# Half-array slots with one PSUM bank per half for the value blocks and a projection of the first nine units of a gated attention kernel

## The chip, the cores and the metric

The kernel runs on one core of one Trainium2 chip. The metric is the device time of one execution in microseconds, the median of several runs; less is better. An engine is named as the profile names it: PE (TensorE's matmuls), PEld (its weight loads), DVE (VectorE), ACT (ScalarE), POOL (GpSimd), SP (SyncE, which issues the DMAs here).

## The reference, cut to what matters

```python
def _A_ref(x, wqkv, wo):                     # x: 1 x 2048 x 512, 32 heads of 16, window 256
    q, k, v = split_heads(x @ wqkv)
    scores = einsum("bhqd,bhkd->bhqk", q, k) * 16 ** -0.5
    scores = where(0 <= i - j < 256, scores, -1e9)
    return merge_heads(softmax(scores) @ v) @ wo

def _B_ref(x, w_gate, w_up, w_down):         # hidden width 1376
    return (sigmoid(x @ w_gate) * (x @ w_up)) @ w_down

g = sigmoid((x * gate_w).sum(-1))
out = g * _A_ref(...) + (1 - g) * _B_ref(...)
```

All data are float32. Every product is computed from operands that are split in a high part (rounded to the fast matmul type fp32r) and a low part (the rest), as high x high + high x low + low x high. So a product over 512 inputs is 4 x 3 = 12 matmuls of 128 rows.

## The kernel before, in words

**Stages.** First x and the weights of the value product are loaded and split, seven of the sixteen value blocks (`v_block`, L416: 128 tokens each) and the first query/key projections (`proj`, L410: 512 tokens of a group of four heads) are computed. Then comes the main loop over `u` (L597). Unit `u` is a block of 128 queries of a group of four heads. For each of the four heads `hh`, `s_part` (L295) computes scores of the queries against at most three blocks of keys, and VectorE finds each row's maximum in one instruction (L311, out `junk`, with a read of the accumulator behind it). Nine units later (`LAG`), with the maxima added in by way of DRAM (`max_split` L318, `max_store`, `max_load`), `st_part` (L343) computes the scores again, transposed and less their maximum, ScalarE takes the exponent, and two units later `pv_part` (L375) adds the product with the values into the bank `pv`. All `s` and `st` matmuls contract over 64 rows only; they use one half of the array's rows, heads 0 and 2 the lower one, 1 and 3 the upper one, so that two of them can run at once. Each takes a bank of `s` (two buffers) or `st` (two buffers; in the first nine units, heads 2 and 3 of `s_part` use those).

**What fills TensorE.** Between the attention matmuls stand those of gate/up and of the projections of later groups (`turns`, L527), in half-array slots: a matmul over 128 rows is cut into one over rows 0 to 63 and one over rows 64 to 127, which add into the same bank (tag `misc`, three buffers) one after the other, 18 slots apart, each beside a half of another group. This starts with unit 9.

**The first nine units** have no `st` and no `pv`. What fills them is a list `first` (L498): the nine value blocks that are left, and the projection 5, appended in unit 5 (L625), 12 slots each. `run_first` (L513) issues them after the four `s_part` of a unit, as whole 128-row matmuls, about 13 per unit. A value block ends with ScalarE's copy from its bank into V (L227; V holds 17 columns per head, the last of them ones); the projection ends with ScalarE's rounding to `sh` and VectorE's low part `sl` (L253, L261), copied by SP's DMAs into the `ring` that the attention reads. In unit 8 the value blocks end, the first gate/up weights are split (L654: they take the place of the value weights), and the projection's 12 matmuls close the stage.

**What sets the order.** PE, ACT, SP and DVE run in the order in which the program calls them. Three lists move work: `behind` (VectorE's steps, emptied after each `s_part` in the first nine units and one per head later), `acts` (ScalarE's), `later` (DMAs). Semaphore waits are put in by the framework wherever a buffer or a value is needed; an instruction that waits holds all that is behind it on its engine.

**The bank `pv`** is cleared at the very start by two matmuls with zeros (L174 to L177), behind 14 others that warm up TensorE (L172), and later by a VectorE memset of 256 columns after each take (L401).

## Time and profile before

| | |
|---|---|
| runs | 753.11 us median of 3 (752.37 to 753.42) |
| the profiled execution | 751.81 us; span of its instructions 750.1 us |
| granted TensorE clock | 1.00 throughout |
| busy share of the span | PE 99%, PEld 78%, DVE 64%, ACT 58%, POOL 23% |
| first instruction to the first s matmul | 0 to 40.94 us |
| units 0 to 8 | 40.94 to 75.16 us |
| first pv matmuls (unit 12) | from 84.83 us |

A row of the trace in order of time has the start in us, the length in us, the engine, the line of the kernel, the operation, out<-in with the shapes, the count, and in brackets the idle time before it with what ended that. Lengths of matmuls overlap, since they are pipelined: their pace is read from one start to the next. Some matmul records are missing from the trace, so rows are picked where the sequence is whole. A row of a stretch has its limits, its length, and the busy time and count of PE, PEld, DVE, ACT and POOL, then the granted clock and the DMA figures. A row of a group has the busy time in us and the mean ns of one behind the bar.

### The profile page before, as it was taken

The numbers are of one execution on the slowest core, as the hardware profiler recorded it, in microseconds if no ns is written. First come the engines' busy times: TensorE is split into PE (matmuls) and PEld (weight loads), VectorE is DVE, ScalarE is ACT, GpSimd is POOL, SyncE is SP. The second block draws the span as 40 slices with busy tenths as digits, with TensorE's granted clock in tenths as the row PEclk, the third lists the DMA queues.
The fourth block names the chain that finished last, engine by engine and source line by source line (L and its number), as shares of the span: only waits on it lengthen the run. The fifth ranks groups of instructions, "written<-read, shape, count | busy, mean of one in ns | idle before, by whom it ended". The sixth has DMA issues, their size and how long they took to land.

```text
span 750.1 us, 17420 instructions
## 1 busy us (share of the span) xinstructions
PE 744.0 (99%) x6180; PEld 581.5 (78%) x6180; DVE 482.0 (64%) x1455; ACT 435.5 (58%) x927; POOL 171.9 (23%) x256
## 2 busy tenths in 40 slices
PE   8999999999999999999999999999999999999997
PEld 6877777787777877778787787778866888888886
DVE  5346767776776766776677676677613776657371
ACT  6422666666676667666667666666656663525241
POOL 7000233233233233323323333332331000000000
PEclk9999999999999999999999999999999999999999
DMA  8340434426344353443543426443355967557451
GB/s 305 96 113 19 105 98 124 127 68 181 113 114 125 109 154 105 122 112 108 153 122 92 125 71 177 125 130 102 109 187 176 290 209 233 170 194 223 128 150 56
DMA packets 69959, 103.58 MB, mean 138 GB/s; under 512 B 19314, under 2 KB 29042, under 8 KB 69872
## 3 DMA queue, kind: packets, MB, share of 16 engines
q1 hardware_dynamic: 69872, 102.48, 46.3%
q8 instruction: 48, 0.79, 0.4%
q14 instruction: 39, 0.32, 0.2%
HBM read 45.26 MB, written 32.00 MB: 103 GB/s over the span
## 4 chain that ended last, share of the span: by engine, by line
PE 97%; DMA 1%; DVE 1%; issue 0%; SPq 0%; ACT 0%; DVEq 0%
PE gu L237 34%; PE pv L384 12%; PE pj L237 11%; PE s L305 7%; PE st L351 5%; PE pd L71 5%; PE pd L73 5%; PE pd L72 5%; PE vps L71 2%; PE pa L73 2%; PE pa L71 2%; PE pa L72 2%; PE vps L73 2%; PE vps L72 2%; DMA V<-in_xT_dram 1%; DVE junk L311 0%
## 5 line engine op out<-in xcount | busy, mean ns | idle before, releaser
L311 DVE CUSTOM_DVE_ANT_0 junk<-s,mask 128x384 f32<-128x384 f32 (+2 forms) x512 | 272.1, 531 | 140.1 <-PE s L305 78.2
L237 PE MATMUL gu<-xh,w 64*128 64x512 f32 (+2 forms) x1384 | 344.4, 392 | 0.0
L356 ACT ACTIVATE pt<-st 128x384 f32<-128x384 f32 (+2 forms) x512 | 242.4, 474 | 169.3 <-PE st L351 69.8
L237 PE MATMUL gu<-xl,w 64*128 64x512 f32 (+3 forms) x692 | 227.4, 392 | 0.0
L237 PEld LDWEIGHTS gu<-xh,w 64*128 64x128 f32 (+2 forms) x1384 | 190.1, 183 | 19.3 <-issue 0.4
L361 POOL TENSOR_SCALAR_AFFINE_SELECT pt<-pt 128x512 f32<-128x512 f32 x128 | 88.1, 688 | 382.3 <-ACT pt L356 382.3
L351 PE MATMUL st<-ring 64*128 64x384 f32 (+2 forms) x536 | 170.2, 332 | 0.0
L305 PE MATMUL s<-ring 64*128 64x384 f32 (+2 forms) x536 | 165.8, 332 | 0.1
L305 PEld LDWEIGHTS s<-ring 64*128 64x128 f32 x536 | 94.4, 184 | 39.3 <-DVE nm L321 12.9
L237 PEld LDWEIGHTS gu<-xl,w 64*128 64x128 f32 (+3 forms) x692 | 107.9, 183 | 5.7
L351 PEld LDWEIGHTS st<-ring 64*128 64x128 f32 x536 | 97.1, 184 | 12.2 <-issue 2.7
L237 PE MATMUL pj<-xh,wqh 64*128 64x512 f32 (+1 forms) x232 | 91.1, 397 | 0.3 <-ACT xh L67 0.2
L384 PE MATMUL pv<-pt,V 128*32 128x384 f32 (+2 forms) x1408 | 91.0, 388 | 0.0
L237 PE MATMUL pj<-xl,wqh 64*128 64x512 f32 (+1 forms) x232 | 90.1, 393 | 0.4 <-DVE xl L68 0.4
L366 POOL TENSOR_SCALAR_AFFINE_SELECT pt<-pt 128x512 f32<-128x512 f32 x112 | 74.2, 663 | 0.0
L237 PE MATMUL pj<-xh,wql 64*128 64x512 f32 (+1 forms) x232 | 70.9, 392 | 0.0
L71 PE MATMUL pd<-ring,hb 128*128 128x512 f32 (+1 forms) x176 | 69.3, 394 | 0.0
L73 PE MATMUL pd<-ring,hb 128*128 128x512 f32 (+1 forms) x176 | 68.9, 392 | 0.0
L72 PE MATMUL pd<-ring,hb 128*128 128x512 f32 (+1 forms) x176 | 68.4, 389 | 0.0
L384 PEld LDWEIGHTS pv<-pt,V 128*32 128x32 f32 x1408 | 37.2, 109 | 36.0 <-issue 29.7
L67 ACT CAST hb<-V 128x512 fp32r<-128x512 f32 (+1 forms) x44 | 27.4, 622 | 63.9 <-DVE V L565 51.4
L479 ACT COPY sp<-gu 128x512 f32<-128x512 f32 (+2 forms) x88 | 51.1, 582 | 2.0 <-PE gu L237 2.0
(74 smaller groups left out, 898.5 us busy)
## 6 DMA issues: line engine op xcount, KB each, us to landing
gu_scratch<-sp SPq DMA_DIRECT2D x80, 256.0 KB
V<-gu_scratch SPq DMA_DIRECT2D x80, 256.0 KB
ring<-sh SPq DMA_DIRECT2D x128, 128.0 KB
ring<-sl SPq DMA_DIRECT2D x64, 128.0 KB
guraw<-in_wgu_dram SPq DMA_DIRECT2D x20, 256.0 KB
V<-in_xT_dram SPq DMA_DIRECT2D x16, 256.0 KB
oT_scratch<-ob SPq DMA_DIRECT2D x128, 32.0 KB
xl<-oT_scratch SPq DMA_DIRECT2D x16, 256.0 KB
```

The source lines that it names most:

```text
L71: mm(ps, lh, rh, start=first, stop=False)
L72: mm(ps, lh, rl, start=False, stop=False)
L73: mm(ps, ll, rh, start=False, stop=last)
L237: mm(pt[0:fw], (wl if w == 2 else wh)[r, d], (xl if w == 1 else xh)[r, d, c * CH:(c + 1) * CH], start=k == 0 and half != 1, stop=k == 3 * ...
L305: mm(pt[:, (k - k0) * P:(e - k0) * P], lhsT, blk(g, k, hh, 1, e - k), start=k == k0, stop=e == i + 1, skip_group_check=True,)
L311: nc.vector.tensor_tensor_reduce(junk[:, 0:n], pt[:, 0:n], mask[:, 3 * P - n:], scale=1.0, scalar=NEG, op0=ALU.add, op1=ALU.max, accum_out ...
L351: mm(pt[:, (q - j) * P:(e - j) * P], lhsT, blk(g, q, hh, 0, e - q), start=q == j, stop=e == last, skip_group_check=True,)
L356: nc.scalar.activation(pts[u][:, hh, 0:n], pt[:, 0:n], AF.Exp, scale=SCALE)
L361: nc.gpsimd.affine_select(p[:, :, 0:P], p[:, :, 0:P], pattern=[[0, HG], [1, P]], compare_op=ALU.is_ge, fill=0.0, base=0, channel_multiplie ...
L366: nc.gpsimd.affine_select(p[:, :, 2 * P:], p[:, :, 2 * P:], pattern=[[0, HG], [-1, P]], compare_op=ALU.is_gt, fill=0.0, base=0, channel_mu ...
L384: mm(pv[32 * hh:32 * hh + 32, (q % 4) * P:(q % 4 + e - q) * P], V[:, j, h * VW:h * VW + 32], p[:, hh, (q - j) * P:(e - j) * P], start=Fals ...
L479: nc.scalar.copy(t[0:width(f, w)], gp.pop((f, c, w))[0:width(f, w)])
```

## The change

1. The two clearing matmuls on `pv` at the start go; the tile is made at unit 9 and cleared there by a VectorE memset of 512 columns. Until then its bank serves as a fourth bank for the value blocks and the projection.
2. A slot of a value block or of projection 5 is now two matmuls, one over rows 0 to 63 and one over rows 64 to 127, each into a bank of its own (`pair_of_banks`: in turn two of the three `misc` banks, and the third with `pv`).
3. The two banks are added: ScalarE copies the lower one to a tile, VectorE adds the upper one to it (`v_sum` into V; `proj_sum` into the tile, after which ScalarE rounds it to `sh` and VectorE computes `sl`).
4. The slots are issued after heads 1 and 3 of each unit (about seven at a time) and no longer all at the unit's end; in unit 8 only two are left for the first place and none for the second.
5. At the end of unit 8 `behind`, `soon` and `behind` are emptied after the projection, so that its sum, its rounding and its low part are in the queues ahead of unit 9.

```diff
-        pv = ps.tile([P, CH], F32, tag="pv", name="pv", bufs=1)
-        for k in range(2):
-            mm(pv[:, 2 * P * k:2 * P * k + 2 * P], warm[:, 0:P], warm[:, 0:2 * P],
-               start=k == 0, stop=True, skip_group_check=True)
...
-        first = [(ND, lambda d, b=b: v_part(b, d), lambda: None) for b in range(vnext, NB)]
+        def pair_of_banks(key):
+            if key not in halves:
+                tags = ("misc", "pv" if len(seen) % 2 else "misc")
+                seen.append(key)
+                halves[key] = [
+                    ps.tile([P, CH], F32, tag=t, name=f"{key}_{i}", bufs=3 if t == "misc" else 1)
+                    for i, t in enumerate(tags)
+                ]
+            return halves[key]
...
+        def v_slot(b, k, half):
+            d, w = divmod(k, 3)
+            r = slice(64 * half, 64 * half + 64)
+            bs = slice(b * P, (b + 1) * P)
+            mm(pair_of_banks(f"vh{b}")[half], (xl if w == 2 else xh)[r, d, bs], (wvl if w == 1 else wvh)[r, d],
+               start=k == 0, stop=k == 3 * ND - 1)
+
+        def v_sum(b):
+            lower, upper = halves.pop(f"vh{b}")
+            t = cpool.tile([P, CH], F32, tag="sp", name=f"vsum{b}", bufs=4)
+            nc.scalar.copy(t, lower)
+            heads = lambda v: v.rearrange("p (h w) -> p h w", w=DH)
+            behind.append(lambda: nc.vector.tensor_tensor(Vh[:, b, :, 0:DH], heads(upper), heads(t), op=ALU.add))
...
+        def proj_sum(s):
+            lower, upper = halves.pop(f"ph{s}")
+            t = cpool.tile([P, CH], F32, tag="sp", name=f"psum{s}", bufs=4)
+            nc.scalar.copy(t, lower)
+            pj[s] = t
+            behind.append(lambda: nc.vector.tensor_tensor(t, upper, t, op=ALU.add))
+            soon.append(lambda: proj_post(s))
...
         def run_first(n):
...
+                k, step, post = going[0]
+                for half in range(2):
+                    step(k, half)
...
             if u == LAG:
...
+                pv = ps.tile([P, CH], F32, tag="pv", name="pv", bufs=1)
+                nc.vector.memset(pv, 0.0)
...
                 if u < LAG:
                     flush(behind)
+                    if hh % 2 == 1:
+                        upto = min(n_first - 3 * ND, n_first * (2 * u + 1 + hh // 2) // (2 * LAG))
+                        run_first(upto - done)
+                        done = upto
...
-            if u < LAG - 1:
-                done += run_first(n_first * (u + 1) // LAG - done)
-            elif u < LAG:
-                run_first(n_first - done - 3 * ND)
+            if u < LAG:
+                flush(soon)
+            if u == LAG - 1:
                 split_gu(0, 0)
                 split_gu(0, 1)
                 flush(acts)
                 flush(behind)
                 run_first(3 * ND)
-                done = 0
+                flush(behind)
+                flush(soon)
+                flush(behind)
```

More of the change, by code (lines that the diff above doesn't have):

```diff
@@ L496, in proj_out, with proj_slot @@
             acts.append(lambda: (proj_hi(s), behind.append(lambda: proj_lo(s))))
-        first = [(ND, lambda d, b=b: v_part(b, d), lambda: None) for b in range(vnext, NB)]
+        halves = {}
+        soon = []
+        def pair_of_banks(key):
[7 more added lines that the diff above has]
+            return halves[key]
+        seen = []
+        def v_slot(b, k, half):
[10 more added lines that the diff above has]
+            behind.append(lambda: nc.vector.tensor_tensor(Vh[:, b, :, 0:DH], heads(upper), heads(t), op=ALU.add))
+        def proj_slot(s, k, half):
+            g, c = divmod(s, NC)
+            d, w = divmod(k, 2) if k < 2 * ND else (k - 2 * ND, 2)
+            r = slice(64 * half, 64 * half + 64)
+            mm(pair_of_banks(f"ph{s}")[half], wq[g][int(w == 2)][r, d], (xl if w == 1 else xh)[r, d, c * CH:(c + 1) * CH],
+               start=k == 0, stop=k == 3 * ND - 1)
+        def proj_sum(s):
[5 more added lines that the diff above has]
+            soon.append(lambda: proj_post(s))
+        first = [
+            (lambda k, h, b=b: v_slot(b, k, h), lambda b=b: v_sum(b)) for b in range(vnext, NB)
+        ]
         rest = [
@@ L513, in run_first @@
         def run_first(n):
-            done = 0
-            while done < n:
+            for _ in range(n):
                 if not going:
                     going.append([0, *(work or first).pop(0)])
-                k, count, step, post = going[0]
-                step(k)
-                done += 3 * ND // count
+                k, step, post = going[0]
+                for half in range(2):
+                    step(k, half)
                 going[0][0] += 1
-                if k + 1 == count:
+                if k + 1 == 3 * ND:
                     going.clear()
                     post()
-            return done
         def turns():
@@ L624, in gated_mix_kernel @@
                 if u < LAG:
-                    first.append((3 * ND, lambda k, s4=s4: proj_mm(s4, k), lambda s4=s4: proj_post(s4)))
+                    first.append((
+                        lambda k, h, s4=s4: proj_slot(s4, k, h), lambda s4=s4: proj_sum(s4)))
                 else:
@@ L658, in gated_mix_kernel @@
                 run_first(3 * ND)
-                done = 0
+                flush(behind)
+                flush(soon)
+                flush(behind)
             if u % 4 == 3 and u < NU:
```

## The prediction

> **What bounds the kernel now.** I read the page's first and fourth parts, then stretches of the trace, then TensorE's, VectorE's and ScalarE's instructions in order of time around the first nine units.

> ```profile
> span 750.1 us, 17420 instructions
> PE 97%; DMA 1%; DVE 1%; issue 0%; SPq 0%; ACT 0%; DVEq 0%
> 40.94:75.16 34.22, 34.22 (x158) 24.51 (x158) 21.34 (x81) 7.44 (x13) 0.00 (x0) 1.00 0.27 73
> ```

> The first two lines are the page's span and its chain by engine; the third is the stretch from the first s matmul to the first of unit 9 (length, then busy time of PE, PEld, DVE, ACT and POOL, granted clock 1.00). PE is never idle there, DVE is busy 21.34 of 34.22 us, ACT 7.44. So TensorE sets the time, and what the change can win must come out of PE's own sequence. In the built programs PE's instructions from unit 9 to the end are the same in the same order; SP's and POOL's are the same throughout. The change can therefore only shift the moment at which the rest begins.

> **What is removed: the seams between full-array and half-array matmuls.** One seam of before, in TensorE's order of time (start, length):

> ```profile
> 48.08 0.40 PE L73 MATMUL vps<-w,xl 128*128 128x512 f32 x1
> 48.41 0.62 PE L305 MATMUL s<-ring 64*128 64x384 f32 x4
> 48.96 0.50 PE L71 MATMUL vps<-w,xh 128*128 128x512 f32 x1
> 49.29 0.39 PE L72 MATMUL vps<-wvl,xh 128*128 128x512 f32 x1
> ...
> 52.09 0.40 PE L72 MATMUL vps<-wvl,xh 128*128 128x512 f32 x1
> ```

> From 49.29 to 52.09 lie twelve steps, 0.23 us each. Across the seam it goes slower: 0.33 before the four s matmuls, 0.55 for them, 0.33 after the first V matmul. What it would be without a seam stands in the later stage, where everything is half-array:

> ```profile
> 300.70 0.33 PE L305 MATMUL s<-ring 64*128 64x384 f32 x1
> 300.87 0.39 PE L237 MATMUL pj<-xh,wqh 64*128 64x512 f32 x1
> 300.87 0.39 PE L237 MATMUL gu<-xh,w 64*128 64x512 f32 x1
> 301.10 0.39 PE L237 MATMUL pj<-xl,wqh 64*128 64x512 f32 x1
> ```

> An s matmul takes its row group 0.17 us, and a pair of 512-column halves starts together and lasts 0.23: as long as one full-array matmul, so a pair costs no more than the one that it replaces. The seam's 1.21 us (48.08 to 49.29) become 0.23 + 2 x 0.17 + 0.23 = 0.80: 0.41 us per unit. For the stage: 120 slots (nine V blocks and one projection, twelve each) x 0.231 = 27.7, two s pairs in each of seven units 14 x 0.175 = 2.45, and four shorter ones, for which I take 0.185, 0.74; together 30.9 against 34.22. **Removed: 3.3 us** (from 0, if half slots keep the loss, to 3.8, if short s matmuls cost next to nothing). s is now issued as two pairs with some seven slots between them; with no seam that costs nothing.

> **What is added on the way: sums of two banks.** ACT copied each V block to V; now it copies one bank to a tile and VectorE adds the other. The nearest rows (groups of the stage, then of the whole span: busy us, mean ns):

> ```profile
> L227 ACT COPY V<-vps 128x512 f32<-128x512 f32 x9 | 5.3, 588 | 24.9 <-PE vps L73 24.9
> L263 DVE TENSOR_TENSOR sl<-pj,sh 128x512 fp32r<-128x512 f32 x1 | 0.7, 692 | 4.7 <-ACT sh L259 4.7
> L777 DVE SCALAR_TENSOR_TENSOR spare<-pa,gs,spare 128x512 f32<-128x512 f32 x16 | 12.0, 751 | 45.3 <-PE pa L73 44.1 <-ACT spare L773 1.2
> ```

> ACT's copy keeps its 0.59 us and has room. No row shows VectorE reading a bank and writing V's spaced rows. I take 0.69 (same operands but for the spacing, which the ACT copy, 588 ns, does not seem to feel), between 0.6 and the dearest of its kind, 0.75. Whether that is hidden is a matter of VectorE's pace:

> ```profile
> 70.06 0.56 DVE L311 CUSTOM_DVE_ANT_0 junk<-s,mask 128x384 f32<-128x384 f32 x1
> ...
> 70.66 0.17 DVE L321 TENSOR_SCALAR nm<-mx 128x16 fp32r<-128x16 f32 x1
> 70.87 0.18 DVE L322 SCALAR_TENSOR_TENSOR nm<-mx,nm 128x16 fp32r<-128x16 f32 x1
> 71.08 0.21 DVE L326 STREAM_TRANSPOSE nt<-nm 128x32 f32<-128x32 f32 x1
> ...
> 73.56 0.56 DVE L311 CUSTOM_DVE_ANT_0 junk<-s,mask 128x384 f32<-128x384 f32 x1
> ...
> 74.27 0.56 DVE L311 CUSTOM_DVE_ANT_0 junk<-s,mask 128x384 f32<-128x384 f32 x1
> ...
> 74.76 1.29 DVE L464 TENSOR_TENSOR w<-guraw,w 128x512 fp32r<-128x512 f32 x2
> 75.96 0.55 DVE L311 CUSTOM_DVE_ANT_0 junk<-s,mask 128x384 f32<-128x384 f32 x1
> ```

> Junk follows junk after 0.71 us, a tensor_tensor follows junk after 0.49, and each of two takes 0.60 until the next may start; max_split makes 0.71 into 1.23. A unit then asks 3 x 0.71 + 0.49 + 0.60 = 3.22 us of VectorE, and 13.3 x 0.231 + 0.35 = 3.43 of TensorE. It fits, with 0.2 to spare: **nothing** is added in units 0 to 8. The cover is thin: at the price 0.75 it still holds; if an add takes over 0.81 of VectorE's time, the rest is paid once per unit. Two banks per group alternate between four, so a group needs the bank of the last but one, given back by that add; it has one group's 2.8 us for it.

> **What is added at the end: a chain before unit 9.** Before, the last projection was rounded by ACT as unit 9 began and its low part came after unit 9's first junk. Now VectorE's order is: two gate/up low parts, the projection's sum, (ACT rounds it), its low part, the memset of the whole pv bank, and only then junk of unit 9, head 0. The third s of unit 9 uses the bank that this junk reads, and PE is in order: all of its later work stands behind it. ScalarE's and TensorE's rows for the steps, and the memset's group (min/median/max ns):

> ```profile
> 75.26 0.59 ACT L259 CAST sh<-pj 128x512 fp32r<-128x512 f32 x1 [1.87 <-PE pj L237]
> 75.16 0.45 PE L305 MATMUL s<-ring 64*128 64x384 f32 x1
> ...
> 78.36 0.44 PE L305 MATMUL s<-ring 64*128 64x384 f32 x1
> L401 DVE MEMSET pv<- x64: 272/272/272, 88.2 to 576.5; 128x256 f32 x64
> ```

> The memset is twice as wide as the row's: between 0.27 and 0.54, taken as 0.5. I count from the start of unit 7's third s, where VectorE has caught up and waits for PE. TensorE: s pair 0.17, six slots, s pair, two slots, s pair, twelve projection slots: 3 x 0.17 + 20 x 0.231 = 5.13, the start of unit 9. Its third s follows two s/st pairs and six slots later, at 6.85. VectorE: junk at 0.4; V add 0.9; junk 1.5; max_split to 2.7; unit 8's junks 2.7, 3.4, 4.1; V add 4.6; junk 5.2; low parts 5.7 and 6.3; projection sum 6.9 to 7.6 (its ACT copy ended at 5.9, not late); ACT rounds to 8.2; low part 8.2; memset 8.8; junk 9.3 to 9.85. The third s waits from 6.85 to 9.9: 3.05 us, and 0.1 for starting again, as 0.33 stands for 0.23 after the seam above. **Added: 3.15 us** (1.8 to 3.6: less if VectorE is not 0.97 late at the sum and the memset takes 0.27, more if adds are dear). In before no such wait stands there: junk of unit 9 ran from 75.96 to 76.5, its third s was due at 75.16 + 1.72. A later wait of 0.3 us in unit 9 (75.16 to 78.36 is 3.20, its work 2.8) is in both.

> On SP the next stack's copies and the reload of the maxima stand behind ACT's rounding: 2.4 us later against PE's end of the projection (8.2 - 5.13 against 75.85 - 75.16), while unit 11, which reads them, starts 3.15 later. Hidden.

> **The start.** Two warm-up matmuls go:

> ```profile
> 1.25 3.35 PE L173 MATMUL warm_ps<-warm 128*128 128x256 f32 x14 [1.25 <-DVE warm L170]
> 4.40 0.63 PE L176 MATMUL pv<-warm 128*128 128x256 f32 x2
> 5.23 0.78 PE L237 MATMUL pj<-xh,wqh 128*128 128x512 f32 x1 [0.19 <-ACT xh L67]
> ```

> The first projection waits for ACT's xh anyway: 0. They ran at 0.24 per 256 columns, half of the later pace; should the 0.6 us of quiet delay the full pace, about four matmuls that do not wait for data lose 0.25 each: 1.0 us, the other end.

> **Sum.** -3.3 + 3.15 = -0.15: 751.81 (span 750.1 and 1.7 around it) becomes about 751.6. The three timed runs of before, median 753.11, lie 0.6 to 1.6 above the profiled execution; the same shift gives 752.9.

> **Rivals.**
> 1. *The handoff is shorter.* VectorE meets the sum on time and the memset is cheap: wait 1.85, gain 1.35, 751.8. To pass 0.2% (1.5 us, about what a measurement of this kernel can tell from no change) one more step of the chain must go, such as ACT's round trip; with no wait at all 749.8. For it: DVE is only 62% busy in the stage before. Against: every step above is in order on one engine.
> 2. *VectorE becomes the bound of units 1 to 8 (slower).* Place: the V add between two junks. It decides from 0.81 us per add; at 1.0 us, eight units lose 0.19 each and the two adds in the chain 0.4 each: 2.3 us in all, 755.3; at 0.9 it is 1.3 us, 754.3. For it: the margin is 0.2 of 3.4 us, and max_split takes half a microsecond twice. Against: every full 128x512 tensor_tensor row here is 0.68 to 0.69. [...]
> 3. *The change does not do what it says:* half slots keep the loss at s, so 0 is removed and the chain stays: 756.3. Against: 300.70 to 301.10 shows no gap.
> 4. *The quiet at the start costs 1.0:* 753.9.

> **How the numbers follow.** Forecast 0.52; rival 1 beyond the bound 0.18; rival 2 0.19; rival 3 0.06; rival 4 0.05. Within 0.2%: 0.52 + 0.05 = 0.57; faster 0.18; slower 0.25. The range takes in half of rival 1 (751.0) and most of rival 2 (755.3); about 0.2 lies outside.

> **What would show it.** Right: s pairs at 0.17 and slots at 0.23 with no 0.33 in the stage, which lasts about 31 us instead of 34.2; one PE wait of about 3 us on DVE at the third s of unit 9; unit 12 starting within 1 us of before. Wrong: PE waits on DVE within units 1 to 8, V adds over 0.8 us, no wait in unit 9, or a first projection that runs slow beyond 8 us.

## The result and the profile after

The changed kernel took 756.91 us (median of 6 runs, 755.53 to 757.50), the kernel before 752.74 beside it (6 runs, 751.85 to 754.69): ratio 1.0049, interval 1.0033 to 1.0066. It is slower by 4.2 us, where 752.9 was forecast. Its profiled execution took 755.64, 3.8 more than the one of before.

From the page of the changed kernel, its span, the chain that ended last by engine, and the row of the granted clock in 40 slices:

```profile
span 753.9 us, 17673 instructions
...
PEclk9999899999999999999999999999999999999999
...
PE 94%; DMA 3%; DVE 1%; ACT 1%; SPq 1%; issue 0%; DVEq 0%; ACTq 0%
```

The one 8 is the fifth slice, 75.4 to 94.2 us: the units just behind the changed stage. Next, stretches of both kernels (length; busy time of PE, PEld, DVE, ACT, POOL; granted clock; DMA). First the changed kernel: from 40.94, where the first s matmul stood before, to unit 9; units 9 to 11; and pieces of these. Then units 9 to 11 of before:

```profile
40.94:71.90 30.96, 30.96 (x279) 26.69 (x279) 25.00 (x88) 7.43 (x13) 0.00 (x0) 1.00 0.31 80
71.90:87.35 15.45, 12.61 (x69) 9.78 (x65) 9.57 (x30) 6.39 (x13) 2.44 (x4) 0.78 0.29 73
...
77.00:78.00 1.00, 1.00 (x7) 0.58 (x4) 0.86 (x4) 0.49 (x1) 0.00 (x0) 0.73 0.29 94
78.00:84.00 6.00, 6.00 (x25) 5.05 (x25) 2.83 (x10) 2.39 (x5) 1.22 (x2) 0.50 0.54 135
84.00:85.00 1.00, 1.00 (x11) 0.81 (x10) 0.16 (x1) 0.19 (x2) 0.87 (x2) 0.85 0.00 0
```

```profile
75.16:84.83 9.67, 9.52 (x67) 7.67 (x67) 7.55 (x26) 5.90 (x12) 2.44 (x4) 1.00 0.46 113
```

The changed kernel's first s matmul starts at 41.10, so its units 0 to 8 last 30.80 us instead of 34.22, with TensorE busy throughout: 3.42 us are won, and unit 9 starts 3.26 earlier. Units 9 to 11 last 15.45 instead of 9.67: 5.78 us are lost. TensorE's instructions in order of time in the changed kernel (start, length) show both. The fence behind them has the first matmul of unit 12 before the change:

```profile
41.10 0.33 PE L301 MATMUL s<-ring 64*128 64x128 f32 x2
...
47.65 0.34 PE L301 MATMUL s<-ring 64*128 64x384 f32 x2
47.83 0.39 PE L513 MATMUL vh<-w,xl 64*128 64x512 f32 x2
48.06 0.40 PE L513 MATMUL vh<-w,xh 64*128 64x512 f32 x2
...
73.40 0.39 PE L233 MATMUL pj<-xl,wqh 64*128 64x512 f32 x1
76.64 0.44 PE L301 MATMUL s<-ring 64*128 64x384 f32 x1 [2.85 <-DVE mx L307]
...
80.14 0.62 PE L233 MATMUL gu<-xh,w 64*128 64x512 f32 x1
80.57 0.62 PE L233 MATMUL gu<-xl,w 64*128 64x512 f32 x1
...
87.35 0.85 PE L380 MATMUL pv<-pt,V 128*32 128x384 f32 x8
```

```profile
84.83 1.16 PE L384 MATMUL pv<-pt,V 128*32 128x384 f32 x9
```

From the s pair to the first slot it is 0.18 us, from there to the next 0.23: the seam is gone. The third s of unit 9 waits 2.85 us for VectorE. Then comes something that the forecast has no term for: from 80.14 there is a 512-column slot every 0.43 us, not every 0.23. TensorE is fully busy and is granted half its clock. The one-microsecond stretches here have a clock of 1.00 or 0.50, all but those at the two ends; so in a row with clock c the share at half pace is 2 x (1 - c): 0.54 us before 78, six to 84, 0.30 after, **6.84 us at half pace, 77.46 to 84.30**. The value product's first matmul, where unit 12 begins, comes at 87.35 instead of 84.83.

The waits of TensorE over the whole execution (line, what it waited for, sum, number, longest):

```profile
PE s L301 <- DVE mx L307: 2.8, 1, 2.8
PE warm_ps L173 <- DVE warm L170: 1.2, 1, 1.2
PE pj L233 <- ACT xh L67: 1.1, 1, 1.1
PE pd L73 <- DVE hb L68: 0.6, 1, 0.6
PE pd L72 <- DVE ring L112: 0.2, 1, 0.2
```

There is no wait within units 1 to 8. The changed kernel is 2.52 us late at unit 12 and still 2.55 late at 577.60, at its last value product. The other 1.3 of the span's 3.8 us arise in the down projection behind 585 (the pd waits are 0.8 of them). Such waits were between 0 and 1.8 us in the kernels below whatever their edit, so they are not put down to the change.

### The profile page after: what moved, and what is told of

Its sections match the earlier page's. It is cut to its first block, busy times and chain, and to the rows that moved or that the text cites. A ratio compares the mean times of both kernels' runs of the same rounds, so it can differ in the third digit from the quotient of the medians.

```text
span 753.9 us, 17673 instructions
## 1 busy us (share of the span) xinstructions
PE 744.1 (99%) x6298; PEld 586.4 (78%) x6298; DVE 487.3 (65%) x1466; ACT 435.2 (58%) x928; POOL 171.9 (23%) x256
## 4 chain that ended last, share of the span: by engine, by line
PE 94%; DMA 3%; DVE 1%; ACT 1%; SPq 1%; issue 0%; DVEq 0%; ACTq 0%
PE gu L233 33%; PE pj L233 12%; PE pv L380 12%; PE s L301 7%; PE st L347 6%; PE pd L71 4%; PE pd L73 4%; PE pd L72 4%; PE vh L513 3%; PE pa L71 2%; PE pa L73 2%; PE pa L72 2%; DMA wdraw<-in_wd_dram 1%; PE vps L71 1%; PE vps L72 1%; PE vps L73 1%
## 5 line engine op out<-in xcount | busy, mean ns | idle before, releaser
L73 PE MATMUL pd<-ring,hb 128*128 128x512 f32 (+1 forms) x176 | 69.1, 392 | 0.6 <-DVE hb L68 0.6
L71 PE MATMUL pd<-ring,hb 128*128 128x512 f32 (+1 forms) x176 | 69.3, 394 | 0.0
L72 PE MATMUL pd<-ring,hb 128*128 128x512 f32 (+1 forms) x176 | 68.5, 389 | 0.2 <-DVE ring L112 0.2
L67 ACT CAST hb<-V 128x512 fp32r<-128x512 f32 (+1 forms) x44 | 27.3, 621 | 64.6 <-DVE V L605 47.1
```

The costliest lines, as they stand in the source:

```text
L71: mm(ps, lh, rh, start=first, stop=False)
L72: mm(ps, lh, rl, start=False, stop=False)
L73: mm(ps, ll, rh, start=False, stop=last)
```

## The experiments

The theory after the result: the wait of 2.85 us is paid twice, once as its length, and once more because TensorE, quiet so long, is granted half its clock for some microseconds after it. Against it: half-array slots by themselves bring the clock down; the missing warm-up matmuls do; or the loss has nothing to do with the clock. "Unit 12" below is the start of the first value product; before, 84.83.

**The same wait, not quiet** (e2): the changed kernel, with twelve half-array matmuls that nobody reads in front of the third s of unit 9.

```diff
+                if u == LAG and hh == 2:
+                    idle = ps.tile([P, CH], F32, tag="misc", name="idle", bufs=3)
+                    for _ in range(12):
+                        mm(idle, wq[1][0][0:64, 0], xh[0:64, 0, 0:CH], start=True, stop=True)
```

> The changed kernel with twelve half-array matmuls, thrown away, ahead of the third s of unit 9: 12 x 0.23 = 2.8 us of work in the wait. The wait's end is VectorE's and stays where it is. Theory 1: the granted clock stays 1.00, unit 12 starts 2.5 to 3.0 us earlier than in the changed kernel, total 753.0 to 754.3. Rival A (the clock falls for another reason than the quiet): clock 0.50 again, total as the changed kernel or up to 2.8 more.

Measured 753.26 us (12 runs), ratio to before 1.0000 (0.9988 to 1.0011). One of the 12 runs had a mean clock of 0.995 (755.67 us), the others 0.997 to 1.000. The stretches of this kernel over the place that has the half pace in the changed one, and two s matmuls behind the filled wait with its unit 12:

```profile
76.00:78.00 2.00, 1.75 (x11) 0.93 (x9) 1.60 (x7) 0.63 (x2) 0.00 (x0) 1.00 0.59 139
78.00:80.00 2.00, 2.00 (x13) 1.78 (x14) 1.68 (x6) 1.34 (x3) 1.23 (x2) 1.00 0.74 193
```

```profile
76.53 0.44 PE L301 MATMUL s<-ring 64*128 64x384 f32 x1
...
77.24 0.44 PE L301 MATMUL s<-ring 64*128 64x384 f32 x1
...
84.41 1.50 PE L380 MATMUL pv<-pt,V 128*32 128x384 f32 x16
```

The handoff on VectorE is as late as in the changed kernel (76.53 against 76.64), only TensorE has something to do meanwhile: the clock stays 1.00, and unit 12 comes 2.94 us earlier. So the lower clock costs 2.9 us in the profiled execution, and without it the change is worth what was forecast, nothing. These 2.9 are less than half of 6.84, since half a clock costs nothing where TensorE is held by VectorE: behind the wait an s matmul comes every 0.71 us with either clock (76.53, 77.24, 77.95 here; 76.64, 77.35, 78.06 in the changed kernel).

**Quiet put into the kernel before** (e6, e7, e10, e11): whole-array slots as before, and 5, 10, 3 and 4 VectorE memsets of an unused tile ahead of unit 9's first junk.

```diff
+                if u == LAG and hh == 0:
+                    idle = cpool.tile([P, CH], F32, tag="ob", name="idle", bufs=2)
+                    for _ in range(5):
+                        nc.vector.memset(idle, 0.0)
```

> The kernel before with five VectorE memsets of 512 columns on an unused tile ahead of unit 9's first junk: a wait of PE of about 1.6 us at the third s of unit 9, and nothing else changed. Theory 1 with a limit above 1.6 us: clock 1.00, 1.5 to 1.8 us slower than before. With a limit below: clock 0.50 for some us and 3 to 5 us slower. Rival A (half slots cause the lower clock): clock 1.00.

> The kernel before with ten such memsets: a wait of PE of about 3.5 us at the third s of unit 9. Theory 1: clock 0.50 for about 6.8 us behind it, 3.5 + 2.8 = 6.3 us slower than before (5.5 to 7). Rival A: clock 1.00 and 3.5 slower.

> The kernel before with three memsets ahead of unit 9's first junk: a wait of PE of about 1.2 us (five gave 2.52, each is 0.66). Theory 1 (quiet beyond a limit lowers the clock): clock 1.00, 1.0 to 1.4 us slower than before. If any such wait lowers the clock: 0.50 for some us and 4 or more slower.

> The same with four: a wait of about 1.9 us. Theory 1: either side of the limit; 1.9 us slower with clock 1.00 in all runs, or 5 to 6 us slower with clock 0.50, or some runs of each kind, if it matters where the wait falls.

Measured: 5 memsets 760.37 (ratio 1.0101, 1.0087 to 1.0116), 10 memsets 763.40 (1.0135, 1.0119 to 1.0150), 3 memsets 758.82 (1.0072, 1.0050 to 1.0093), 4 memsets 759.81 (1.0088, 1.0064 to 1.0112). The wait and the stretches around it with three memsets:

```profile
78.84 0.53 PE L305 MATMUL s<-ring 64*128 64x384 f32 x1 [1.20 <-DVE mx L311]
```

```profile
79.00:80.00 1.00, 1.00 (x5) 0.90 (x6) 0.86 (x3) 0.49 (x1) 0.00 (x0) 0.52 0.56 107
80.00:89.00 9.00, 9.00 (x40) 7.34 (x39) 3.96 (x14) 2.83 (x6) 2.44 (x4) 0.50 0.30 81
89.00:90.00 1.00, 1.00 (x10) 0.86 (x10) 0.56 (x2) 0.49 (x1) 0.00 (x0) 0.86 0.00 0
```

Half-array slots in units 0 to 8 aren't needed for the effect. But the expectation that a short wait leaves the clock alone fell: 1.20 us of quiet brought 0.96 + 9 + 0.28 = 10.24 us at half pace, more than the 2.85 us of the changed kernel did. Five and ten memsets cost 7 and 10 us where at most 5 and 7 were expected; their waits were longer than foreseen too, 2.52 and 5.81 us instead of 1.6 and 3.5. And with four memsets the clock fell only 2.1 us after the end of the long wait. Rows of that kernel, its waits and its stretches:

```profile
78.98 0.44 PE L305 MATMUL s<-ring 64*128 64x384 f32 x1 [1.86 <-DVE mx L311]
80.77 0.45 PE L305 MATMUL s<-ring 64*128 64x384 f32 x1 [0.27 <-DVE mx L311]
```

```profile
81.00:82.00 1.00, 1.00 (x6) 0.80 (x5) 0.86 (x3) 0.55 (x2) 0.87 (x2) 0.53 0.76 193
82.00:87.00 5.00, 5.00 (x23) 4.11 (x21) 1.83 (x8) 1.47 (x3) 0.74 (x2) 0.50 0.16 43
87.00:88.00 1.00, 1.00 (x9) 0.80 (x6) 0.35 (x1) 0.31 (x1) 0.83 (x2) 0.55 0.00 0
```

**The chain shortened step by step** (e3: the value product's bank made and cleared in unit 10; e12: the two gate/up low parts behind unit 9's junks), both from the changed kernel.

```diff
e3
             if u == LAG:
...
+            if u == LAG + 1:
                 pv = ps.tile([P, CH], F32, tag="pv", name="pv", bufs=1)
-                nc.vector.memset(pv, 0.0)
+                behind.append(lambda: nc.vector.memset(pv, 0.0))
e12
-                flush(behind)
...
-                flush(behind)
+                behind.pop()()
                 flush(soon)
-                flush(behind)
+                behind.pop()()
```

> The changed kernel with pv made and cleared in unit 10 behind a junk, the rest of the chain kept: the wait shrinks by 0.4 to 0.5 us to about 2.4. Theory 1 with a sharp limit between 2.4 and 2.85: clock 1.00, total 753 to 754. Theory 1 with a limit below 2.4: clock 0.50 again and a gain of 0.5 only, 755.5 to 756.5.

> The changed kernel with the two gate/up low parts put behind unit 9's junks, the projection's sum, rounding, low part and the memset still ahead of them: the wait shrinks by 0.9, since ScalarE's copy then sets the sum's start, to 1.9 to 2.1 us. Clock 1.00: 751.5 to 752.5, faster than before. Clock 0.50: 754.5 to 755.5.

Measured: e3 756.52 (4 runs, 1.0047, 1.0032 to 1.0062), e12 756.62 (9 runs, 1.0041, 1.0028 to 1.0054): neither is clearly better than the changed kernel (1.0049), and e12 is slower than it was expected to be with either clock. Both shorten the wait, to 2.27 us and to the two in these rows of e12:

```profile
76.33 0.44 PE L301 MATMUL s<-ring 64*128 64x384 f32 x1 [2.08 <-DVE mx L307]
78.49 0.44 PE L301 MATMUL s<-ring 64*128 64x384 f32 x1 [0.64 <-DVE mx L307]
```

and in both the clock still falls. The loop begins at different times in these executions (first s matmul at 40.94 before, 41.10 in the changed kernel, 42.18 in e3, which also has half pace at its start, from 8.28 to 11.70). So the length of units 9 to 11, from unit 9's first s to the first value product, is compared. All kernels with such a wait, the half pace worked out from one-microsecond stretches as above:

| kernel | wait, us | half pace from, to | its length | units 9 to 11, beyond 9.67 | wait plus half of the half pace outside it |
|---|---|---|---|---|---|
| changed | 2.85 | 77.46, 84.30 | 6.84 | 5.8 | 6.3 |
| e12 | 2.08 and 0.64 | 78.80, 85.62 | 6.82 | 6.0 | 6.1 |
| e3 | 2.27 | 76.56, 86.80 | 10.24 | 6.4 | 7.1 |
| e10, 3 memsets | 1.20 | 79.04, 89.28 | 10.24 | 5.7 | 6.3 |
| e11, 4 memsets | 1.86 and 0.27 | 81.06, 87.90 | 6.84 | 5.6 | 5.5 |
| e6, 5 memsets | 2.52 | 78.64, 88.88 | 10.24 | 6.4 | 7.0 |
| e7, 10 memsets | 5.81 | 79.20, 92.86 | 13.66 | 9.9 | 10.5 |

The last column is the price if TensorE sets the pace all through the half clock. In e11 and e12, where the clock falls when the waits are over, it holds within 0.1 us. In the other five the loss is 0.5 to 0.7 us smaller. For the changed kernel the s matmuls 0.71 us apart, at VectorE's pace, show why; for the other four this was not worked out.

**Nothing of the chain ahead of unit 9** (e1; e5 with 16 warm-up matmuls instead of 14): gate/up low parts, the rounding and the memset all go behind unit 9's and unit 10's junks, one per head; stack 2's copies start a unit later.

```diff
-                flush(behind)
...
-                flush(behind)
-                flush(soon)
-                flush(behind)
+                behind.insert(0, behind.pop())
+                acts.extend(soon)
+                soon.clear()
```

> The changed kernel with the work before unit 9 put off: the projection's sum, its rounding, its low part, the gate/up low parts and the memset of pv are called one per head from unit 9 on, behind the junk of that head (and the stack's copies one unit later). Theory 1 (VectorE's chain makes the third s of unit 9 wait 2.85 us, and that quiet lowers TensorE's granted clock to 0.50 for 6.8 us): no PE wait on DVE over 0.6 us in unit 9, granted clock 1.00 throughout, unit 12 some 3.0 us earlier than in before, 749.3 to 750.3 us. Rival A (half slots themselves bring the lower clock, by what they ask of TensorE): the clock falls all the same and the time stays above 752. Rival B (the loss is at the end, where the down projection's loads come late): unit 12 is earlier, but the end is still 1 us or more late.

> The version with everything put off, and with sixteen warm-up matmuls in place of fourteen, as many as before had with its two clearing ones. Theory 1 with a second, smaller effect at the start (the 0.6 us of quiet sometimes lowers the clock for 3.4 us behind the warm-up, as one profile showed, 1.1 us late at the first s): no run with a lower clock at the start, median 0.3 to 1.0 us below that version, 750.0 to 750.7. Rival (the start does not matter, the first xh is what is waited for): the same median within 0.2.

Measured: e1 751.00 (5 runs, ratio 0.9968, 0.9956 to 0.9980), e5 750.94 (7 runs, 0.9969, 0.9959 to 0.9980). Unit 12 of e1:

```profile
82.39 1.50 PE L380 MATMUL pv<-pt,V 128*32 128x384 f32 x16
```

The clock stays at 1.00 in these units, and unit 12 starts 2.4 us earlier than before. The expectation had 3.0 us and at most 750.3; the rest is several pauses of up to 0.3 us between TensorE's starts in units 9 and 10, where VectorE now has most to do. Two warm-up matmuls more or less make no difference: their removal had no part in the loss. A half pace at the start is in the profiled executions of e3, with 14 warm-up matmuls (3.42 us, see above), and of e7 and e8, with 16 (in e7 two of these are the clearing ones): their clock over the first 10 us is 0.88 and 0.90.

**Parts alone** (e4: the kernel before with its slots split behind head 1 and head 3, so nine seams more; e8: as e1, but with the projection whole-array as before, the stack's copies not put off, and 16 warm-ups).

```diff
e4
+                    if hh == 1:
+                        done += run_first(min(n_first - 3 * ND, n_first * (2 * u + 1) // (2 * LAG)) - done)
e8
-                        lambda k, h, s4=s4: proj_slot(s4, k, h), lambda s4=s4: proj_sum(s4)))
+                        lambda k, h, s4=s4: h or proj_mm(s4, k), lambda s4=s4: proj_post(s4)))
```

> The kernel before with the slots of units 0 to 8 put half behind head 1 and half behind head 3, still whole-array: nine seams more (s pairs stand alone eighteen times). If a seam costs 0.35 to 0.41 us whatever it holds: 3.0 to 3.7 us slower than before, all within units 0 to 8. Rival (the 3.3 us that the stage gained come from the finer placing, not from the missing seams): the same or faster than before.

> The change with the value blocks alone as half slots: projection 5 stays whole-array with ScalarE's rounding as before, gate/up low parts and the memset of pv behind unit 9's and 10's junks, sixteen warm-up matmuls. It saves VectorE one sum (0.6 us) and ScalarE a copy, and costs two changes of mode, about 0.4 us. Theory 1: clock 1.00, no PE wait on DVE over 0.6 us, 749.5 to 750.8. If VectorE is still the limit of units 9 to 11 in the version with everything put off, this one is the faster by 0.2 to 0.5.

Measured: e4 756.53 (4 runs, 1.0042, 1.0029 to 1.0055). Its first value product:

```profile
87.85 1.50 PE L384 MATMUL pv<-pt,V 128*32 128x384 f32 x16
```

It starts 3.0 us later for nine seams more, 0.33 each, and the removed ones were 3.42 for nine units. So the seam is what the change wins. e8: 751.46 (11 runs, 0.9978, 0.9967 to 0.9988), slower than the 749.5 to 750.8 expected and not faster than e1, so sparing VectorE the projection's sum brought nothing that shows. It still keeps some two thirds of e1's gain: most of it is in the value blocks.

**The chain spread out** (e9): the changed kernel, with each VectorE step put behind a junk of a later unit, no earlier than its result is wanted: the projection's sum in unit 9, the first gate/up low part in unit 10, the memset in unit 11, the rest in unit 12. Stack 2's copies start a unit later, as in e1.

```diff
+                gu_low = behind[:]
...
+                soon.clear()
+                plan = {
+                    (9, 1): behind.pop(), (10, 1): gu_low[0], (11, 1): lambda: nc.vector.memset(pv, 0.0),
+                    (12, 1): lambda: proj_lo(5), (12, 2): gu_low[1],
+                }
```

> The changed kernel with the work before unit 9 spread thinly: projection sum behind the second junk of unit 9, rounding with its third head, first gate/up low part in unit 10, memset of pv in unit 11, low part of the projection and second gate/up low part in unit 12; fourteen warm-up matmuls. Theory 1: no wait over 0.3 us and clock 1.00; unit 12 about 3.2 us earlier than in before (81.4 to 81.9) where the version with all put off had 82.4, since VectorE is asked for 1.8 us less in units 9 to 11; 749.6 to 750.6. If those waits in units 9 to 11 do not come from VectorE's extra work: 82.4 and 751 again.

Measured **748.66 us** (5 runs, 748.49 to 750.00), ratio 0.9943 (0.9927 to 0.9959): faster than both kernels, and than the 749.6 to 750.6 expected. The stretches of this kernel over the place where the changed one falls to half pace, its unit 12, and TensorE's waits over the whole execution:

```profile
76.00:78.00 2.00, 2.00 (x16) 1.75 (x16) 1.80 (x6) 1.24 (x3) 1.06 (x2) 1.00 0.64 145
78.00:80.00 2.00, 2.00 (x21) 1.94 (x19) 1.57 (x7) 0.98 (x2) 1.11 (x2) 1.00 0.66 154
```

```profile
81.70 1.18 PE L380 MATMUL pv<-pt,V 128*32 128x384 f32 x12
```

```profile
PE warm_ps L173 <- DVE warm L170: 1.2, 1, 1.2
PE pj L233 <- ACT xh L67: 0.9, 1, 0.9
PE pd L72 <- DVE ring L112: 0.4, 1, 0.4
```

TensorE no longer waits for VectorE at s, the clock is 1.00, and unit 12 starts 3.13 us earlier than before, although the loop began 0.52 later in this execution (41.46): all of the seams' gain is kept. The profiled execution ended only 2.1 earlier than that of before, while the medians of the runs differ by 5.1. The runs of before spread by 3.7 us beside it, those of e9 by 1.5, so what lies beyond 3.1 is not ascribed.

## Why the prediction was wrong

- **What bounds the kernel, the seams (-3.3): right.** 3.42 measured; s pairs 0.17 to 0.18, slots 0.23, the stage 30.8 where 30.9 was added up.
- **Sums of two banks, hidden: right.** The group of the nine V sums has 0.69 us each, as taken, and no TensorE wait lies in units 1 to 8, where the margin was 0.2 per unit:

```profile
L521 DVE TENSOR_TENSOR V<-vh,vsum 128x512 f32<-128x512 f32 x9 | 6.2, 686 | 0.0
```

  Rival 2, VectorE as the bound, thus didn't come about.
- **The chain ahead of unit 9: right in every step.** VectorE's instructions in the changed kernel, from the last V sum to unit 9's first junks:

```profile
71.19 0.69 DVE L521 TENSOR_TENSOR V<-vh,vsum 128x512 f32<-128x512 f32 x1
71.80 0.55 DVE L307 CUSTOM_DVE_ANT_0 junk<-s,mask 128x384 f32<-128x384 f32 x1
72.27 1.29 DVE L460 TENSOR_TENSOR w<-guraw,w 128x512 fp32r<-128x512 f32 x2
73.47 0.68 DVE L535 TENSOR_TENSOR psum<-ph,psum 128x512 f32<-128x512 f32 x1
74.84 0.69 DVE L259 TENSOR_TENSOR sl<-psum,sh 128x512 fp32r<-128x512 f32 x1 [0.68 <-ACT sh L255]
75.64 0.48 DVE L642 MEMSET pv<- 128x512 f32 x1
76.03 0.54 DVE L307 CUSTOM_DVE_ANT_0 junk<-s,mask 128x384 f32<-128x384 f32 x1
```

  They are two low parts, the sum, 0.68 of waiting for ACT's rounding, the low part, the memset of 0.48 (0.5 taken) and the junk. The wait was 2.85 where 3.05 was worked out.
- **"Added: 3.15 us": this step failed.** It takes the wait at its length and 0.1 for starting again, and puts the clock behind the wait at nothing without a reason. Units 9 to 11 lost 5.78: 2.85 of wait, and 2.9 because TensorE then had half its clock for 6.84 us. The bounds 1.8 to 3.6 held the wait and not its price. e2 shows the missing part by itself: with the wait filled, the sum of the prediction holds (ratio 1.0000).
- **Rivals 1 and 3 fell too:** the handoff was only 0.2 us shorter than worked out, and half slots keep no seam. That rival 3's 756.3 lies near the measured 756.9 is chance.
- **The start at nothing: right** (e5 750.94 against e1 751.00). There, rival 4 even supposed a quiet that delays the full pace, but only the one of 0.6 us at the start; it wasn't asked of the wait of 3 us that the prediction itself put into the middle. The row of the warm-up was at hand, which shows 0.24 us per 256 columns, half of the later pace, where nothing had run before (the clock of that stretch, 1.25 to 4.40, reads 1.00 all the same).
- **The run's own spread.** Mean granted clock over a run is 0.995 in three of the changed kernel's six runs and 0.991 to 0.992 in the other three, 0.997 to 1.000 in all runs of before in the experiments. One stretch of 3.41 us at half pace takes 3.41 / 2 / 754 = 0.0023 off that mean and costs up to 1.7 us, half its length. So the profiled execution, with two, is one of the cheaper ones, and three others by their mean have up to four. That can be a part of why the medians lie 4.2 apart where unit 12 lies 2.5 later; those runs have no trace that would show it.

## What to carry to other kernels

Before work is put ahead of a point where TensorE waits for another engine, ask what half pace may follow, and price the wait at its length plus that: in units 9 to 11, waits of 1.2 to 5.8 us cost 2.9 to 4.5 us more. So shortening such a wait from 2.85 to 2.27 us (e3), or to 2.08 and 0.64 (e12), brought nothing; how short it must be was not tried between 0.3 and 1.2 us. Spreading the same steps over the next units, each behind a head's own work, took away both prices (e9). Where whole-array and half-array matmuls alternated, a seam cost about a third of a microsecond each time (0.33 in e4, 3.42 for nine units in the changed kernel). Cutting the whole-array ones into halves saved it; VectorE had room to add the two banks here, at 0.69 us each.

## What the runs showed of the hardware

In the 3.41 us ahead of each fall TensorE was idle for 1.17 us (e6), 1.20 (e10), 1.45 (e7), 1.58 (e12), 1.60 (e11), 1.69 (e3) and 2.59 (changed kernel); the 3.41 us ahead of these, with 1.14 us idle (e12) and 0.53 (e11), were followed by full pace. An idle share of about a third as the limit would fit these nine; that is an estimate from them alone, which no run was made to test. A wait of 1.30 us in e4's down projection, between whole-array matmuls, is longer than e10's, and the clock stayed at 1.00 (580 to 620):

```profile
602.87 0.50 PE L73 MATMUL pd<-ring,hb 128*128 128x512 f32 x1 [1.30 <-DVE hb L68]
```

In e6 the same wait, for `hb` at L73, is 1.8 us long, and the clock over 580 to 620 is 0.96. So a wait's length alone does not tell whether the clock falls. Whether it matters that the matmuls around a wait are half-array or whole-array ones is open; no run was made to test it.

The length of the half pace follows in part from the wait. In e3, e6 and e7 its first steps of 3.41 us still hold quiet of the wait (0.59 us in e3, 1.35 in e6, 3.41 and 0.94 in e7), and behind the last of these come two more. In the changed kernel, e11 and e12 there are two from the start, with TensorE busy. Why there are two and in e10 three, but about one at the start of e3, e7 and e8 and in e6's down projection, where the matmuls use the whole array, stays open.

VectorE memsets of one tile right behind each other start 0.66 us apart. Each takes 0.48, as the lone one, and waits 0.17 for the one before it, which writes the same tile; e6:

```profile
77.05 0.48 DVE L638 MEMSET idle<- 128x512 f32 x1 [0.17 <-DVE idle L638]
```

That is a part of why the waits of e6 and e7 were longer than expected.
